# Row groups, PSUM ring and issue orders in the front of a two-layer spectral mixer

## The chip, the cores and the metric

The kernel runs on one core of a Trainium2 chip. The core has TensorE (PE, matrix multiplies), VectorE (DVE), ScalarE (ACT), GpSimd (POOL) and SyncE (SP, which here only issues transfers). The metric is the device time of one execution in microseconds (us), the median of three runs. The profile's span, 346.4 us, runs from the first to the last instruction and is some 2 us shorter than the time of a run.

## The reference

The input x is one sequence of 2048 rows by 512 features in bf16. Two layers follow each other, each of two halves:

```python
x = x + _A_ref(_layernorm(x), A_w_r, A_w_i)      # irfft2(rfft2(x) * W)
x = x + _B_ref(_layernorm(x), B_w1, ..., B_w4)
# _B_ref: h  = gelu(layernorm(x) @ w1)           512 -> 512
#         x1 = x + shifted(h) @ w2               four column groups, shifted by -1, +1, -2, +2 rows
#         y  = x1 + gelu(layernorm(x1) @ w3) @ w4   512 -> 1792 -> 512
```

Both layers use the same weights. The two-dimensional Fourier transforms are done as matrix multiplies with cosine and sine tables.

## The kernel before

**Layout.** A row number of the sequence is written as 16 p + q. The partition is p (128 of them), and q (0 to 15) counts what the code calls a row: a block of 128 x 512. All of x stays on the chip in `x_state`.

**Front.** The first transform needs the normalized x. The mean takes no part in it, except at one frequency, and the scale 1/std of a row is folded into the table: for every row q the engines take statistics (`s`), form mean and variance (`i`), take a square root on ACT for a group of rows (`S`, line 375), invert it on DVE (`J`, line 378), and scale the table T by it (`Q`, line 393 on DVE, line 395 on ACT). PE then multiplies the row with its scaled table (`O`, function `over_p_quarters`, line 424, eight matmuls a row), and a copy takes the result out of PSUM into `V` (`G`, line 157 on DVE, line 159 on ACT). Rows in `ON_ACT` get their statistics from two passes on ACT (lines 363 and 299) and a little arithmetic on GpSimd (`f`, lines 369 to 371); the others from `bn_stats` and `bn_aggr` on DVE (lines 287 and 315). `GROUPS` says which rows share one root. `FIRST` pairs the rows for PE and the copies. Two rows a pair take two PSUM banks; the last two rows go singly, row 15 into two half banks that ACT and DVE empty side by side.

**PSUM.** There are eight banks. In the front `banks` (line 146) hands them out from a ring of six. In the layers every order names its bank after a point (`d0.3` is bank 3), so the ring plays no part there. Zero matmuls (`wake` and `fill`, line 271) in bank 7 keep PE busy before there is data; `WAKE` is how many.

**Layers.** The layers' stages are: second transform step (`d`, line 542 to 548 in layer 1, 553 in layer 2), third step (`q`, 577), the weighting with W on DVE (`p`, 596), the way back (`b` 607, `D` 625, `P` 637), the residual (`a`, 645), layernorm, `w1` (`v`, 677), `w2` (`u`, 693), layernorm, `w3` (`w`, 728), `w4` (`W`, 748), residual (`A`, 754). Before `w1` and `w3` SyncE transposes rows by DMA (`T` and `U`, line 665). Layer 1's last stage already contains the front of layer 2 (`S`, `J`, `Q`, `O`, `G` again).

**Order.** The order is written by hand. `ORDER_0`, `ORDER_A` (layer 1) and `ORDER_B` (layer 2) are lists of such letters with a row, group or pair number and, where there is a choice, V or A for the engine. Each engine takes its own instructions in the order in which the list names them; dependencies between engines become semaphore waits. So moving a letter matters only as against the letters of the same engine, or where it changes who wrote a buffer last.

**Transfers.** SyncE loads x in eight parts and then W; GpSimd loads the tables FL, TL and TR after `f` of group `TABLES` (line 206) and then copies W's rows into the odd partitions, gated by the last scaled table (line 204). Late in the front SyncE queues the MLP weights and layer 2's table FA (line 224), and after layer 1 the table G2 (line 213).

Of the kernel before, what the change touches and what calls it, by code (L numbers as in the profile page):

```python
# [13 lines left out]
BF16 = dt.bfloat16  # L14
# [131 lines left out]
def banks(K, n):  # L146

    k = K.bank
    if k is None:
        k = K.next_bank if K.next_bank + n <= 6 else 0  # L150
        K.next_bank = (k + n) % 6
    return K.ps[:, k:k + n, :]


# [7 lines left out]
def load_all(K, A_x, A_w_r, A_w_i, B_w1, B_w2, B_w3, B_w4):  # L162
    nc = K.nc
    tabs = dft_tables()
    dram = {k: nc.inline_tensor(v, name="tab_" + k).ap() for k, v in tabs.items()}

    def table(k, eng):
        t = K.const.tile(list(tabs[k].shape), BF16, name=k)
        eng.dma_start(t[:], dram[k])
        setattr(K, k, t)  # L170
# [39 lines left out]
        load_TR(1)  # L210

    K.load_tables, K.load_rest = load_tables, load_rest
    K.load_G2 = lambda: nc.sync.dma_start(K.G[:], dram["G2"])

    def load_mlp():
        gate2 = K.const.tile([1, 16], BF16, name="gate2")
        nc.sync.dma_start(gate2[:], K.W[1:2, 1, NH - 1, 1:17])
        for k in ("G", "Tinv"):
            table(k, nc.sync)
        for k, w, n, c in (("w1", B_w1, 4, D), ("w2", B_w2, 4, D), ("w3", B_w3, 4, FH), ("w4", B_w4, 14, D)):  # L220
            t = K.const.tile([P, n, c], BF16, name=k)
            nc.sync.dma_start(t[:], w.rearrange("(t p) n -> p t n", p=P))
            setattr(K, k, t)
        table("FA", nc.sync)

    K.load_mlp = load_mlp
    K.eps = K.const.tile([P, 1], FP32, name="eps")
# [30 lines left out]
def wake(K):  # L258
# [6 lines left out]
    K.zeros = t  # L265
    fill(K, WAKE)


def fill(K, n):
    for i in range(n):  # L270
        K.nc.tensor.matmul(K.ps[:, 7 if K.bank is None else K.bank, 0:256], lhsT=K.zeros[:], rhs=K.zeros[:].unsqueeze(1).to_broadcast([P, 2, P]), start=True, stop=True)
# [126 lines left out]
def over_p(K, qs, split=False):  # L398

    ps = banks(K, 2 if split else len(qs))  # L400
    for i, q in enumerate(qs):
        Tq = K.Tq.pop(q)
        for t in range(2):
            o = ps[:, t, 0:256] if split else ps[:, i, t * 256:(t + 1) * 256]
            a, z = t * P, 256 + t * P
            K.nc.tensor.matmul(o, lhsT=K.x[:, q, a:a + P], rhs=Tq[:, 0:1].to_broadcast([P, 2, P]), start=True,
                               stop=False)
            K.nc.tensor.matmul(o, lhsT=K.x[:, q, z:z + P], rhs=Tq[:], start=False, stop=True)
    return ps
# [53 lines left out]
def first_front(K):  # L463

    new_V(K)
    K.Tq = {}
    at = {q: (g, i) for g, rows in enumerate(GROUPS) for i, q in enumerate(rows)}
    L = [Stats(K, n=len(rows)) for rows in GROUPS]
    for g, rows in enumerate(GROUPS):
        if any(q in ON_ACT for q in rows):  # L470
            L[g].sums()
# [4 lines left out]
    def stats(q):  # L476
        g, i = at[q]
        if q in ON_ACT:
            L[g].mean(i, K.x[:, q, :])
# [22 lines left out]
    def means(g):  # L502
        for i, q in enumerate(GROUPS[g]):
            if q in ON_ACT:
                L[g].from_means(i)
        if g == TABLES:
            K.load_tables()
# [343 lines left out]
PLAIN = 5  # L851
FLEX = "mGnotxY"
ORDER_0 = """
s0 s3 s2 i3 s1 f0 i0 i2 S0 s5 f1 J0 Q0V Q1V Q2A Q3A s4 i4 s6 s7 i6 i7 O0 G0A S1 s10 J1 s12 Q6A s9 Q7V s13 i12 i13 Q4V
s8 S3 O1 G1A Q5V O3 J3 O2 i10 G3A Q12V s11 i8 i11 Q13V O6 f2 S2 J2 G2A Q10V Q11V Q8V O5 G6A Q9A O4 s15 s14 i15 i14 S4
J4 Q14V O7 G5A Q15V G4A O8 G8A G7V G8V
"""
ORDER_A = """
d0.3 t0V d1.6 d2.0 t1A q0.2 x0V p0 t2A q1.4 x1A p1 d4.6 N0 t4A d10.1 t10A q2.4 x2V p2 q4.6 d6.0 x4A t6A d12.3 t12A
d14.5 q10.6 q6.0 d8.2 p4 x10A b4.4 x6V b3.7 d15.6 t8A q8.2 m4A t15A p10 p6 q12.0 b1.4 m3A b0.6 b2.7 x8A x12A b6.2 m2A  # L860
t14V b5.3 m1V p8 q15.0 m0A q14.4 b10.7 x15A b9.6 p12 m6A m10V p15 b8.0 m5A x14A b7.2 m7A b11.3 p14 b12.7 m8V b13.5 m9V
b14.1 m11A m12A b15.2 m13A m14A X4.0 m15A m15V D1.5 Y1A D0.0 Y0A D3.3 Y3A P2.5 a2 s2 P3.6 a3 s3 P0.0 a0 P7.2 P1.7 s0
P6.5 D2.0 a1 s1 a7 s7 r0 a6 s6 Y2V e0 i0 n1V D5.6 Y5A n0V T0 D4.2 Y4A P4.0 a4 P5.4 a5 s4 n3V D7.5 s5 r1 Y7A n2V P11.3
P8.7 c0 a8 a11 e1 i1 n4V n5V T1 P10.4 a10 D6.0 Y6A s8 s10 P15.5 T2 P14.3 n7V n6V s11 P9.2 P12.0 a9 s9 P13.4 c1 v0.1
v1.6 r2 c2 a13 h0 L9 a12 h1 T3 v3.0 a15 n10V s15 v2.5 n11V T5 n8V n9V a14 h3 u0.7 f0 s13 E0 h2 u3.1 T4 s12 f3 E3 u1.6
s14 r3 f1 n15V v5.0 h5 k0 n14A v4.4 h4 n12V n13V T6 u2.7 f2 k2 E2 u4.1 k3 u5.2 f5 c3 u6.0 f6 k1 k6 E1 u7.6 f7 T7 v6.4
f4 h6 R0 o0A o1V U0 o2V v7.3 h7 u13.5 u8.1 u12.6 L12 f8 u10.0 f10 E10 o3A u11.3 U1 f11 E11 E6 u15.7 f12 k7 k12 u9.4
w1.2 E8 f13 g1 L4 k4 E5 f9 E9 w0.0 g0 w5.5 w2.0 g5 w4.5 E13 k5 R1 L13 o5V E4 L10 o6V E7 g2 w3.1 g3 g4 f15 w6.3 g6 k10
W0.2 A0 o7A W3.0 A3 L1 o4A W1.3 A1 U3 U2 w10.1 g10 k8 B1 k9 j1 B3 w7.4 g7 w11.6 W2.0 A2 B2 E15 k11 B0 L3 k13 R2 o10V
o9A o11V w12.2 g12 u14.4 f14 j2 j3 j0 S0 Q0 Q3 g11 w8.0 g8 k14 w9.3 Q1 g9 k15 L8 w13.6 g13 W6.4 A6 U5 W7.2 E12 z0 o8A  # L870
A7 W4.3 U4 w16.4 g16 A4 w15.6 g15 L14 R3 o13V w18.4 g18 w19.0 g19 o12V B4 w14.6 g14 Q2 w20.4 w17.2 W5.6 L6 o15A g20
L11 A5 g17 W9.2 E14 o14V U6 W8.7 O1.3 G1A G1V B5 j5 U7 j4 A8 W10.6 A10 B6 j6 w22.3 g22 B7 W11.0 j7 B8 S1 w24.3 Q5 Q6
A9 B9 g24 j8 L0 L5 O0.1 G0A L2 w23.5 A11 G0V B11 g23 w27.3 j11 B10 g27 w21.6 j10 Q7 g21 j9 w26.3 S2 Q10 g26 w25.1 Q4
Q11 O3.4 g25 Q8 L15 Q9 O2.6 G2A G2V G3A G3V W12.3 A12 B12 j12 S12 W15.6 A15 B15 j15 S15 J15 W13.3 Q15 J12 A13 B13 j13
Q12 W24.4 A24 B24 S13 J13 Q13 W14.5 A14 B14 O4.6 O15.2 G4A j14 S14 G15A G15V O5.4 G5A O6.1 J14 Q14 O14.3 G6A G4V X3.5
G14V X4.0 G14A L7
"""
ORDER_B = """
d15.7 t15V d4.1 t4V d1.3 t1A d8.6 q1.4 x1V t8A p1 q4.2 x4A q15.0 x15V p4 d12.4 t12A d10.6 q8.2 p15 q12.4 t10A x12A
b1.0 d14.1 t14A d2.6 m1A t2A x8V p8 d0.2 p12 b5.5 m5A t0A q10.0 q2.3 x2A x10V p10 d6.5 t6A b9.2 b4.1 b12.0 q14.6 q0.4  # L880
m9A q6.2 m12A p2 m4A b11.0 x0V p0 x6A p6 b2.1 m2A b10.4 x14A b8.2 m8A m10A p14 b3.1 m3A b0.7 m0V b7.5 m11A b13.3 m13A
b14.6 b6.2 m6A m7V m14V b15.4 m15A m15V D3.0 Y3A D2.4 Y2V D1.6 Y1A P6.0 a6 s6 D0.2 Y0A P4.4 a4 s4 P5.5 a5 P7.6 a7 s5
P2.1 P1.4 a2 P0.2 a0 a1 s7 P3.6 a3 r1 D5.0 s2 s0 e1 i1 n5V n4V T2 D7.2 n6V n7V T3 D4.4 Y4V Y5A P11.1 P10.0 a10 s3 s1
r0 Y7A e0 D6.6 i0 P9.5 n2V P8.2 n3V T1 Y6A a11 s10 n0V P14.3 n1A P13.0 P15.7 P12.1 a9 s11 s9 a8 s8 T0 a14 s14 a15 a13
v2.4 r2 v3.2 h3 h2 n9V v1.6 h1 v0.2 u3.5 a12 s12 n8V T4 c0 h0 u1.4 n10V s15 u0.3 c1 n11V f1 f3 T5 s13 f0 E0 k1 k0 r3
n13V u2.6 n15A v5.4 n12V n14V c2 h5 v4.0 f2 E2 E1 u4.5 f4 h4 k4 u7.6 k3 k2 T6 R0 f7 k7 u5.4 f5 u6.7 k5 T7 v6.1 E5 v7.3
h6 h7 o2A o0V E7 o1V c3 u12.2 E3 o3V u8.4 u14.5 f8 u10.1 f14 u15.0 f12 E8 U0 f6 u13.5 f13 k13 U1 w1.3 g1 k8 E6 w5.5 g5
w3.3 E13 k6 f10 g3 w0.1 g0 E14 k10 w6.4 g6 f15 k15 E15 k12 w2.6 g2 k14 w4.4 g4 u11.7 R3 f11 E12 W0.6 o15A o12V o13A
o14V W2.4 U6 u9.1 f9 E9 R1 o5A W3.5 o7V A0 U7 w21.0 w24.6 A3 w27.2 g21 g24 o6A g27 E4 W1.7 A1 w22.2 A2 y2 g22 w26.0
g26 w23.3 g23 z0 w25.6 g25 E10 E11 o4V W12.0 y0 U2 U3 w11.2 g11 w10.6 g10 w13.2 g13 k9 A12 W13.1 k11 R2 o8V o9V o10V  # L890
w7.4 W14.7 A13 w12.2 A14 w9.0 g9 y3 y13 U4 g12 w8.6 g8 W15.1 A15 g7 W4.5 A4 W5.6 A5 y4 y1 W6.3 A6 o11A U5 w14.5 g14 y5
y12 w17.1 g17 y6 w15.4 g15 w18.1 g18 w20.4 g20 w16.0 g16 w19.5 g19 W8.3 A8 y8 W9.2 A9 W7.4 A7 y15 y7 W10.6 A10 y9
W11.5 A11 W20.6 y11 y14 y10 A20 y20
"""


# [28 lines left out]
```

## Time and profile before

Three runs took 348.36, 348.44 and 348.58 us; the median is 348.44 us. The profiled run took 348.18 us.

| engine | busy us | share of the span |
|---|---|---|
| PE | 338.0 | 98% |
| ACT | 198.0 | 57% |
| DVE | 186.0 | 54% |
| POOL | 62.3 | 18% |

A timeline line reads: start, duration, engine, line of the kernel, operation, output tile, input tiles, shapes, how many were merged; in brackets the idle time of the engine before it and what ended that. PE's busy time includes the pipelined ends of matmuls, so successive matmuls overlap in it. A line that merges several instructions gives the time from the first start to the last end. A windows line gives a stretch, its length, then busy us and instruction count of PE, weight loads, DVE, ACT and POOL, the granted share of the PE clock, the busy share of the DMA engines and GB/s.

Where PE stands still: 1.01 us at the start, 1.02 and 0.80 us in the front, 0.21 and 0.16 us as layer 1 begins, some 1.0 us between 180 and 222 us, and from the end of the last matmul, 342.70 us, to the end of the span.

### The profile page before, as it was taken

The page shows a single profiled execution, that of the slowest core. Times are in us where ns is not written, and L with a number is a line of the kernel's source. Part 1 is how long each engine was busy: PE and PEld are TensorE (multiplying, and loading weights), DVE is VectorE, ACT ScalarE, POOL GpSimd, SP SyncE. Part 2 cuts the span into 40 slices and gives each one's busy share as a digit, 9 for nine tenths or more (in the row PEclk, how much of TensorE's full clock was granted, in tenths as well). Part 3 has the DMA queues.
Part 4 walks back from the last instruction along what each step waited for, and adds up shares of the span by engine and source line. Part 5 has one row for each costly group of instructions (what it writes and reads, how often), then busy time and mean ns, then how long its engine had stood idle before and what let it go on. Part 6 is the DMA issues. An engine that isn't in the chain of part 4 may idle for free.

```text
span 346.4 us, 5700 instructions
## 1 busy us (share of the span) xinstructions
PE 338.0 (98%) x2181; PEld 190.4 (55%) x2181; DVE 186.0 (54%) x445; ACT 198.0 (57%) x351; POOL 62.3 (18%) x160
## 2 busy tenths in 40 slices
PE   7999999999999999999999999999999999999995
PEld 5778884444444444444577888444444444444453
DVE  4979597668343451178789969766523110211021
ACT  5989899765616616015537979976581444132500
POOL 2460047520301400010000002653022001000000
PEclk9999999999999999999999999999999999999999
DMA  7987985430030301300000002543003070203002
GB/s 263 285 298 237 383 221 105 78 63 1 3 61 0 62 5 26 62 1 1 2 0 2 2 2 45 101 87 64 10 2 61 0 108 0 45 24 84 0 32 77
DMA packets 45547, 25.12 MB, mean 73 GB/s; under 512 B 34976, under 2 KB 42272, under 8 KB 45520
## 3 DMA queue, kind: packets, MB, share of 16 engines
q1 hardware_dynamic: 44048, 20.27, 24.3%
q0 software_dynamic: 1232, 4.40, 3.7%
q8 instruction: 17, 0.28, 0.3%
q10 hardware_dynamic: 240, 0.10, 0.2%
q14 instruction: 10, 0.08, 0.1%
HBM read 12.13 MB, written 2.10 MB: 41 GB/s over the span
## 4 chain that ended last, share of the span: by engine, by line
PE 80%; DVE 8%; ACT 7%; DMA 2%; issue 2%; DVEq 0%; ACTq 0%
PE ps L748 28%; PE ps L728 28%; PE ps L693 8%; PE ps L677 7%; DVE ln_st L287 2%; PE ps L625 2%; PE ps L607 2%; ACT xn L299 2%; PE ps L637 1%; DVE PB L596 1%; ACT V L159 1%; ACT hT L159 1%; PE ps L577 1%; DVE X L157 1%; ACT X L159 1%
## 5 line engine op out<-in xcount | busy, mean ns | idle before, releaser
L735 ACT ACTIVATE gT<-ps 128x1024 bf16<-128x1024 f32 x56 | 56.7, 1024 | 81.1 <-PE ps L728 80.4
L748 PE MATMUL ps<-w,gT 128*128 128x512 bf16 (+1 forms) x476 | 99.2, 366 | 0.0
L728 PE MATMUL ps<-xT,w 128*128 128x512 bf16 x448 | 99.1, 379 | 0.0
L748 PEld LDWEIGHTS <-gT 128*128 128x128 bf16 x476 | 46.5, 98 | 50.1
L728 PEld LDWEIGHTS <-w 128*128 128x128 bf16 x448 | 43.8, 98 | 52.6
L754 DVE TENSOR_TENSOR x_state<-ps,x_state 128x512 bf16<-128x512 f32 (+1 forms) x34 | 22.2, 657 | 87.0 <-PE ps L748 87.0
L701 DVE SCALAR_TENSOR_TENSOR xn<-xn,ln_c,ps 128x512 bf16<-128x512 bf16 x32 | 23.5, 745 | 27.3 <-PE ps L693 24.1
L693 PE MATMUL ps<-w,hT 128*128 128x512 bf16 x128 | 29.2, 379 | 0.0
L677 PE MATMUL ps<-xT,w 128*128 128x512 bf16 x128 | 28.8, 379 | 0.1
L299 ACT ACTIVATE junk<-xn 128x512 bf16<-128x512 bf16 x32 | 19.9, 622 | 13.3 <-DVE xn L701 13.3
L645 DVE SCALAR_TENSOR_TENSOR x_state<-ps,x_state 128x512 bf16<-128x512 f32 x32 | 20.5, 685 | 4.3 <-PE ps L637 4.1
L287 DVE BATCH_NORM_STATS2 ln_st<-x_state 128x6 f32<-128x512 bf16 (+1 forms) x30 | 19.7, 664 | 3.5 <-DMA x_state<-in_A_x_dram 3.2
L693 PEld LDWEIGHTS <-hT 128*128 128x128 bf16 x128 | 12.4, 98 | 15.3 <-ACT hT L684 0.8
L677 PEld LDWEIGHTS <-w 128*128 128x128 bf16 x128 | 12.4, 98 | 15.3 <-issue 0.7
L305 POOL TENSOR_SCALAR ln_mv<-ln_s 128x4 f32<-128x4 f32 x16 | 5.7, 359 | 82.0 <-DVE x_state L645 68.7
L299 ACT ACTIVATE xn<-x_state 128x512 bf16<-128x512 bf16 x32 | 20.0, 632 | 0.4 <-DVE x_state L645 0.2
L596 DVE TENSOR_TENSOR PB<-X,W 128x2048 bf16<-128x2048 bf16 (+1 forms) x20 | 19.4, 1009 | 0.2
L684 ACT ACTIVATE hT<-ps 128x512 bf16<-128x512 f32 x32 | 17.4, 604 | 2.5 <-PE ps L677 2.4
L307 POOL TENSOR_TENSOR ln_mv<-ln_s,ln_t 128x4 f32<-128x4 f32 x16 | 3.6, 225 | 78.5 <-ACT junk L299 71.4
L607 PE MATMUL ps<-TR,PB 128*128 128x128 bf16 x256 | 16.3, 219 | 0.3 <-DVE X L157 0.3
L159 ACT ACTIVATE TV<-ps 128x1024 bf16<-128x1024 f32 (+1 forms) x16 | 14.2, 913 | 4.0 <-PE ps L553 2.3
L625 PE MATMUL ps<-G,hT 128*128 128x256 bf16 x128 | 15.3, 273 | 0.6 <-ACT hT L159 0.5
(96 smaller groups left out, 389.7 us busy)
## 6 DMA issues: line engine op xcount, KB each, us to landing
w<-in_B_w_dram SPq DMA_DIRECT2D x2, 1792.0 KB, 13.1
W<-W POOLq DMA_DIRECT2D x4, 514.0 KB, 5.5
x_state<-in_A_x_dram SPq DMA_DIRECT2D x8, 256.0 KB, 4.8
out_dram<-x_state SPq DMA_DIRECT2D x15, 128.0 KB, 1.8
w<-in_B_w_dram SPq DMA_DIRECT2D x2, 512.0 KB, 5.4
W<-in_A_w_r_dram SPq DMA_DIRECT2D x7, 128.5 KB, 6.7
W<-in_A_w_i_dram SPq DMA_DIRECT2D x7, 128.5 KB, 6.4
TL<-tab_TL POOLq DMA_DIRECT2D x3, 256.0 KB, 4.8
```

The lines of the kernel that those rows point to most:

```text
L159: K.nc.scalar.activation(dst, src, ACT.Copy, bias=0.0, scale=1.0)
L287: self.K.nc.vector.bn_stats(self.st[i][:, int(k)], src)
L299: K.nc.scalar.activation(out, src, ACT.Square, bias=0.0, scale=D ** -0.5, accum_out=self.s[:, i, 1:2])
L596: nc.vector.tensor_tensor(t, X.pop(u)[:, 0:2 * n].unsqueeze(1).to_broadcast([P, 2, 2 * n, 256]), K.W[:, :, 2 * u:2 * u + 2 * n, 1:257], op ...
L607: nc.tensor.matmul(oh, lhsT=pab[u][:, k, 2 * (b - u) + h, F * P:(F + 1) * P], rhs=K.TR[:, k:k + 2, 2 * b + h], start=(k == 0), stop=(k == 1))
L625: nc.tensor.matmul(o[:, i, e * 256:(e + 1) * 256], lhsT=M[:, F, e, 2 * m + i, :], rhs=K.G[:, F, e, :], start=(F == 0 and e == 0), stop=(F ...
L677: nc.tensor.matmul(o[:, i], lhsT=K.w1[:, t, j * P:(j + 1) * P], rhs=xT[g][:, :, t, :], start=(t == 0), stop=(t == 3))
L693: nc.tensor.matmul(o, lhsT=K.hT[:, j, st:st + P], rhs=K.w2[:, j, :], start=(j == 0), stop=(j == 3))
L701: nc.vector.scalar_tensor_tensor(xn[:, q, :], xn[:, q, :], ln[q // 4].c[:, q % 4:q % 4 + 1], ps.pop(("u", n)), op0=ALU.mult, op1=ALU.add, ...
L728: nc.tensor.matmul(o[:, i], lhsT=K.w3[:, c, t * P:(t + 1) * P], rhs=xT3[g][:, :, c, :], start=(c == 0), stop=(c == 3))
L735: nc.scalar.activation(gT[g][:, 2 * j:2 * j + 2, :], ps.pop(("w", k)), ACT.Gelu_apprx_tanh, bias=0.0, scale=1.0)
L748: nc.tensor.matmul(o, lhsT=gT[g][:, t, i * P:(i + 1) * P], rhs=K.w4[:, t, d], start=(t == 0), stop=(t == 13))
```

## The change

The front gets smaller groups at its start (rows 0 and 1, then 2 and 3), so that a first root does not have to wait for four rows; row 1's statistics go to DVE, so that rows 5 and 9 alone are on ACT. The ring gets all eight banks, so that PE can be one pair further ahead of the copies. Pairs 5 and 6 are copied by DVE and pairs of earlier rows by ACT. Of the zero matmuls three are taken out. The tables FL, TL and TR are loaded after group 2, which now holds rows 4 to 7. FA and G2, layer 2's tables, are each loaded in two halves, one for each of their two index values, so that a reader depends on its half alone. The three orders are written anew; in the two layers' lists most entries keep their places, and the cut diff below shows the moves that touch an engine's own sequence.

```diff
     k = K.bank
     if k is None:
-        k = K.next_bank if K.next_bank + n <= 6 else 0
-        K.next_bank = (k + n) % 6
+        k = K.next_bank if K.next_bank + n <= 8 else 0
+        K.next_bank = (k + n) % 8
...
-    K.load_G2 = lambda: nc.sync.dma_start(K.G[:], dram["G2"])
+
+    def load_G2():
+        for f in range(2):
+            nc.sync.dma_start(K.G[:, f], dram["G2"][:, f])
+
+    K.load_G2 = load_G2
...
-        table("FA", nc.sync)
+        K.FA = K.const.tile(list(tabs["FA"].shape), BF16, name="FA")
+        for t in range(2):
+            nc.sync.dma_start(K.FA[:, t], dram["FA"][:, t])
...
-WAKE = 30
+WAKE = 27
-GROUPS = [[0, 1, 2, 3], [4, 5, 6, 7], [8, 9, 10, 11], [12, 13], [14, 15]]
-ON_ACT = [1, 5, 9]
-TABLES = 1
+GROUPS = [[0, 1], [2, 3], [4, 5, 6, 7], [8, 9, 10, 11], [12, 13], [14, 15]]
+ON_ACT = [5, 9]
+TABLES = 2
...
 ORDER_0 = """
-s0 s3 s2 i3 s1 f0 i0 i2 S0 s5 f1 J0 Q0V Q1V Q2A Q3A s4 i4 s6 s7 i6 i7 O0 G0A S1 s10 J1 s12 Q6A s9 Q7V s13 i12 i13 Q4V
-s8 S3 O1 G1A Q5V O3 J3 O2 i10 G3A Q12V s11 i8 i11 Q13V O6 f2 S2 J2 G2A Q10V Q11V Q8V O5 G6A Q9A O4 s15 s14 i15 i14 S4
-J4 Q14V O7 G5A Q15V G4A O8 G8A G7V G8V
+s0 s1 s3 i1 i0 s2 s4 i3 i2 S0 J0 Q0V s5 i4 S1 J1 Q1A O0 s6 s7 i6 i7 s8 Q2A Q3A O1 f2 S2 J2 i8 Q6V Q7V s9 f3 s10 O3 Q4V
+Q5A s11 O2 G0A i10 i11 s13 S3 G1A J3 Q8V Q10A Q11A Q9V O4 s12 i13 i12 S4 G3A s15 s14 J4 i15 i14 Q12V S5 Q13V G2A G4A
+J5 Q14V O5 Q15V O6 G5V O7 G7A G6V O8 G8A G8V
...
 ORDER_A = """
-... Y7A n2V P11.3 P8.7 c0 ...
+... Y7A n2V P8.7 P11.3 c0 ...
-... u15.7 f12 k7 k12 u9.4 w1.2 ...    W1.3 A1 ...    w7.4 g7 w11.6 W2.0 ...    w21.6 ...
+... u15.7 k7 f12 k12 w1.2 u9.4 ...    W1.4 A1 ...    W2.0 A2 ... w11.6 ...    w21.5 ...
...
 ORDER_B = """
-... D6.6 i0 P9.5 n2V P8.2 ...    u5.4 ...    u12.2 E3 o3V u8.4 u14.5 ...    o15A o12V o13A o14V W2.4 ...
+... D6.6 i0 n2V P8.2 P9.5 ...    u5.3 ...    u14.5 o2A E7 o1V c3 u12.2 ...    o15A o13V o14V W2.4 o12V ...
-... W10.6 A10 y9 W11.5 A11 W20.6 y11 y14 y10 A20 y20
+... W10.6 A10 y10 y9 W11.5 A11 W20.6 y11 y14 A20 y20
```

Besides these, some residual adds (`E`), permutations of W (`L`), norms (`o`) and table scalings (`Q`) change places among DVE's or ACT's instructions of the stages in which PE works through w2, w3 and w4.

## The prediction

> **What bounds the kernel now.** I read the windows by stage first, then the waits of each engine, then the chain of waits inside the stages where TensorE (PE) is not full. The windows view gives start:end, length, and busy us of each engine:
>
> ```profile
> 4.00:20.00 16.00, 13.79 (x148) 11.71 (x147) 13.63 (x45) 13.65 (x29) 7.02 (x17) 1.00 0.99 327
> 20.00:38.00 18.00, 17.96 (x259) 14.95 (x257) 16.80 (x21) 17.17 (x27) 3.87 (x6) 1.00 0.80 272
> 38.00:47.00 9.00, 8.70 (x78) 7.49 (x78) 5.36 (x17) 8.00 (x19) 1.06 (x5) 1.00 1.06 369
> 47.00:180.00 133.00, 133.00 (x688) 65.31 (x687) 78.79 (x206) 67.82 (x120) 26.72 (x63) 1.00 0.19 35
> ```
>
> From 47 to 180 us PE never stops: orders of VectorE (DVE) and ScalarE (ACT) there can save nothing, only create a wait. Where the change can pay is the front, 4 to 20 us, in which PE, DVE and ACT are all at about 85%, none full. DVE's timeline shows its idle times in brackets, with what ended them:
>
> ```profile
> 6.79 0.18 DVE L378 RECIPROCAL ln_r<-ln_r 128x4 f32<-128x4 f32 x1 [0.43 <-ACT ln_r L375]
> 14.53 0.18 DVE L378 RECIPROCAL ln_r<-ln_r 128x4 f32<-128x4 f32 x1 [0.25 <-ACT ln_r L375]
> 17.19 0.17 DVE L378 RECIPROCAL ln_r<-ln_r 128x2 f32<-128x2 f32 x1 [0.36 <-ACT ln_r L375]
> 18.67 1.15 DVE L157 CAST V<-ps 128x512 bf16<-128x512 f32 x2 [0.72 <-PE ps L424]
> ```
>
> PE's timeline of the front:
>
> ```profile
> 7.34 2.80 PE L424 MATMUL ps<-Tq,x_state 128*128 128x256 bf16 x32 [1.02 <-DVE Tq L393]
> 10.94 8.36 PE L424 MATMUL ps<-Tq,x_state 128*128 128x256 bf16 x96 [0.80 <-ACT Tq L395]
> 19.51 0.22 PE L542 MATMUL ps<-xT,V 128*128 128x128 bf16 x1 [0.21 <-ACT V L159]
> 19.88 0.23 PE L544 MATMUL ps<-xT,V 128*128 128x128 bf16 x1 [0.16 <-DVE V L157]
> ```
>
> So from 10.94 PE runs its last 12 rows almost without a gap, 8.1/12 = 0.67 us a row, and DVE waits 0.72 us for it at the end. The layer begins at 19.88, when the last DVE copy out of PSUM is done. The number to forecast is that moment, and what later waits do with it. At the other end stands the store:
>
> ```profile
> 337.45 6.28 SPq L758 DMA_DIRECT2D out_dram<-x_state  x6
> 342.74 0.42 DVE L754 TENSOR_TENSOR x_state<-ps,x_state 128x256 bf16<-128x256 f32 x1 [0.84 <-PE ps L748]
> ```
>
> The last add ends at 343.16; taken one by one, the last three issues before the final one start at 341.93, 342.31 and 342.79 (row 10's first half), and the final store at 343.33.
>
> [...] full clock is recorded from 4.85 us on, through idle times of 1.02 and 0.80 us; no longer idle stands in it. [...] Banks 6 and 7 are not in the front's ring before (bank 7 takes only the zero matmuls), so the longer ring needs nothing else.
>
> **The change part by part.**
>
> *Rows 0 and 1.* Row 1's statistics move from ACT (two passes, 1.23 us of its queue from 4.17) to DVE. DVE start-to-start times, from its timeline: statistics 0.60 (15.33 to 15.94), aggregate 0.10, scaling of T 0.20, reciprocal 0.08, or 0.21 if its scaling follows at once; a 128x1024 copy from PSUM lasts 1.22 us, so 1.14 less the 0.08 overlap of neighbours. These reproduce a stretch without waits: from 7.40 to the last scaling at 14.02 are 8 statistics, 8 aggregates, 2 reciprocals, 4 scalings: 6.56 us against 6.62.
>
> *DVE's new sum.* 14 statistics 8.40, 14 aggregates 1.40, six reciprocals (three of each kind) 0.87, ten scalings 2.00, two whole copies (pairs 5 and 6, before on ACT) 2.28, the half row at the end 0.43: 15.38 us. Before: 13 statistics, 13 aggregates, five reciprocals, twelve scalings, a 512 and a 256 copy: some 13.5 us of work plus 1.76 us of waits and short tails. DVE thus gets 1.9 us more work and must lose its waits. Walking its queue: statistics of 0, 1, 3 from 4.17; of 2 at 6.18; of 4 at 6.78, when its load (landed 6.45) is there; the first reciprocal at 7.58, its ACT root done at 6.64; row 0's scaling 7.79 to 8.07. Reciprocal 1 at 8.1 (ACT root 7.76 to 8.06, behind row 5's two passes). Reciprocal 2 at 10.2, 3 at 12.98, 4 at 15.59: each root is ready before. Reciprocal 5 waits about 0.1 us: row 14's aggregate ends 15.93, root 16.03 to 16.33. Scalings 14 and 15 at 16.6 and 16.8, copies at 17.0 and 18.15, last copy 19.2 to 19.65. Without any wait 4.17 + 15.38 = 19.55.
>
> *PE.* Row 0 starts at about 8.1, not 7.34. At 0.66 us a row: rows 0 to 3 end at 10.7 (row 1 waits for ACT's scaling to 8.5); rows 6, 7 from 10.76; row 4 from 12.07; row 8 from 13.5 (scaled at 13.44); rows 10, 11 to 16.1; rows 12 to 15 from 16.13 to 18.8, against about 19.2 now. The later start is thus regained, since row 6 comes at 10.76 where now the second run starts at 10.94.
>
> *ACT.* Two rows of passes 2.5, six roots 1.2, six scalings at 0.41 2.5, five whole copies at 0.92 4.6, a 512 and a 256 copy about 1.0: 11.8 us against about 13. Walked, it ends near 19.2 (19.38 now). Its copies free the ring in time: bank 2 at 13.7 for a pair ready at 14.8, bank 4 at 15.7 for 16.13, bank 6 at 17.15 for 17.45, bank 0 at 18.06 for 18.1; the last is a tie. With six banks pair 4 would wait for pair 0's copy and so on by one pair earlier; this is what the ring buys, and it is in the walk.
>
> **Front: last copy ends at 19.65 instead of 19.82: -0.2 us**, bounds 19.4 (PE end 18.8 + 0.2 + 0.43) and 19.9 (0.1 us of wait at each of three more roots).
>
> *27 zero matmuls.* At full clock each takes 0.109 us, so they end 0.33 us earlier; PE then idles to 8.1, some 2.0 us. [...] I take 0 and keep 1.5.
>
> *Tables on GpSimd after means 2.* Row 5's second pass ends at 7.9 us in both orders (it is group 1 before and group 2 after), so the loads issue at 8.7 as now. The turn of TL waits for the last scaling, 17.0 instead of 17.95, and lasts 2.6: ready at 19.7, needed at 21.0. Zero.
>
> *20 to 47 us.* I sorted both orders by engine: up to the first back_p the sequences of PE, DVE, ACT and GpSimd are the same; only the interleaving in the text moves. So the stage should shift whole. The doubled W for row pair 0 lands at 21.07 and is used at 22.41; the table work ahead of it issues no later. -0.2 passes through.
>
> *FA in two loads.* SyncE's queue:
>
> ```profile
> 33.38 8.22 SPq L169 DMA_DIRECT2D FA<-tab_FA  x1
> 41.70 1.70 SPq L518 DMA_TRANSPOSE xT<-zeros  x1
> 47.40 12.72 SPq L665 DMA_TRANSPOSE xT<-xn  x6
> ```
>
> The issue of FA blocks for 8.22 us, and behind it stand the dummy transpose and the first transposes of the layer, for which w1(0) at 52.7 waits. A second issue like Tinv's costs 0.47 us and the slack is 47.40 - 43.40 = 4 us: zero. If the second blocked until the weights have landed (48.2), the transposes would slip 2 to 3 us and w1(0), whose second transpose lands at 52.3, by 2 us. G2's second load adds 0.5 us at 145, with the next transpose at 213: zero.
>
> *Orders of the layers.* PE: back_p 8 before 11, w3 swaps, one w2 earlier, two other banks; no operation added. Their producers are done: over 45 to 346 us PE's own waits in the trace sum to 1.0 us, none at these places. In layer 2 norm3 of row 13 goes from ACT (0.80) to DVE (0.41): transpose 6 earlier, but its pair lands at 264.8 and w3(21) starts at 267.0, so hidden. Zero, bounds ±0.3.
>
> *Last stores.* Row 10's half store leaves the place before the final one (issue 0.45). The final store can go when its add is done, 343.16 + 0.04, not at 343.33: -0.13.
>
> **Sum:** 348.44 - 0.2 - 0.13 = 348.1 us.
>
> **The rivals.** (a) *PE sets the front's end and DVE's waits vanish fully*, with better filled ACT queues in 20 to 38 us, where ACT is at 95%: -0.4 there, -0.13 at the tail and another 0.4 from 20 to 47, 347.5. For it: DVE's four waits; against: the later orders are the same by engine. (b) *DVE becomes the bound and loses*: each group of two rows makes its own trip DVE, ACT, DVE of about 0.7 us (6.06 to 7.00); if two of the six are exposed as the three now are, +0.7 - 0.2 - 0.13, and a tie on bank 0 adds 0.2: 349.0. (c) *A stall*: [...] blocked FA, 349.8 to 350.2; against it [...] 4 us of slack.
>
> **How the numbers follow.** The forecast has 0.58, (a) 0.23, (b) 0.12, (c) 0.07. The range 347.4 to 348.9 holds the forecast with its bounds, (a) and the nearer half of (b). Faster by over 0.7 us (0.2%): (a) and a little of the forecast, 0.26; slower by over 0.7: most of (b) and (c), 0.17; the rest, 0.57, is within.
>
> **What would show it.** DVE without brackets from 4.17 to the last copy; PE's first row at 8.1 and last at 18.8; L544 first at about 19.7; 20 to 47 us shifted whole; final store at 343.2 less the shift. Wrong if PE rows of the front take 1.3 us, if a transpose waits behind FA, or if a PE wait appears between 47 and 180 us.

## The result, and the profile after

The change makes the kernel a little faster: 347.34 us (median of 6, 347.02 to 347.96) against 348.51 us for the kernel before beside it (6, 348.17 to 349.55). The ratio is 0.9962, with a 95% interval of 0.9945 to 0.9979, so 1.17 us were gained where 0.34 were forecast. A further series, `after_b`, gives the same size: 0.9961 (0.9949 to 0.9974). In another, `after_again`, 11 executions at the full clock of TensorE have a median of 347.32 us, but 10 had a mean granted clock of 0.993 to 0.995 and took 1.5 us longer; over these 21 the ratio is 0.9981 (0.9969 to 0.9993), so there the change is worth about half as much. (One more execution of that series, at a clock of 0.75, took 443.23 us and is left out.) The lower clock of 0.993 to 0.995 came in 17 of 71 executions with the new front on that chip, in none of 112 with the old front there, and, `after_ring6` apart, in none of 37 with the new front on the three other chips of the experiments.

The windows of the same four stages, in the changed kernel (columns as before):

```profile
4.00:20.00 16.00, 13.76 (x146) 11.75 (x145) 15.06 (x47) 11.81 (x27) 7.29 (x15) 1.00 0.98 324
20.00:38.00 18.00, 17.94 (x258) 14.82 (x255) 16.84 (x21) 17.32 (x27) 2.86 (x5) 1.00 0.90 306
38.00:47.00 9.00, 8.76 (x79) 7.63 (x80) 5.49 (x16) 8.00 (x19) 1.06 (x5) 1.00 0.97 321
47.00:180.00 133.00, 132.58 (x682) 65.39 (x688) 78.91 (x207) 67.69 (x120) 27.87 (x63) 1.00 0.19 34
```

In the first line VectorE (DVE) goes from 13.63 to 15.06 busy us of 16 and ScalarE (ACT) from 13.65 to 11.81: work has moved from ACT to DVE, and DVE is now nearly full. In the other three lines the busy times of VectorE and ScalarE differ by at most 0.15 us and those of PE by at most 0.42 of 133, so whatever came later cannot be seen in busy time. DVE's timeline of the front has one bracket before the last copy of V, the wait for x at its start:

```profile
4.42 1.88 DVE L294 BATCH_NORM_STATS2 ln_st<-x_state 128x6 f32<-128x512 bf16 x3 [3.47 <-DMA x_state<-in_A_x_dram]
...
16.98 2.68 DVE L157 CAST V<-ps 128x1024 bf16<-128x1024 f32 x3
20.21 0.69 DVE L157 CAST TV<-ps 128x512 bf16<-128x512 f32 x1 [0.54 <-PE ps L555]
```

The four waits that stood there before (0.43, 0.25, 0.36, 0.72 us) are gone. TensorE (PE) has one unbroken run of 128 matmuls:

```profile
1.01 5.37 PE L278 MATMUL ps<-zeros 128*128 128x256 bf16 x27 [1.01 <-DVE zeros L269]
8.19 10.95 PE L431 MATMUL ps<-Tq,x_state 128*128 128x256 bf16 x128 [1.80 <-DMA x_state<-in_A_x_dram]
19.48 0.22 PE L549 MATMUL ps<-xT,V 128*128 128x128 bf16 x1 [0.35 <-ACT V L159]
19.72 0.23 PE L551 MATMUL ps<-xT,V 128*128 128x128 bf16 x1
```

SyncE's queue, where FA is now two issues in one line:

```profile
32.46 9.34 SPq L231 DMA_DIRECT2D FA<-tab_FA  x2
41.90 1.20 SPq L525 DMA_TRANSPOSE xT<-zeros  x1
47.25 12.88 SPq L672 DMA_TRANSPOSE xT<-xn  x6
```

**Where the time came from.** When x arrives is not in the kernel's hands: the first statistics start anywhere from 4.08 to 4.50 us over the traces of this study. So stages are compared by their own lengths. Both columns are from traces in which w1's first product does not wait for a transpose: the kernel before, and `after_look2`, the changed kernel in a further execution.

| stretch | before, us | after, us | difference |
|---|---|---|---|
| first statistics to the end of V's last copy | 15.65 | 15.24 | -0.41 |
| from there to the first back_d product | 18.39 | 18.39 | 0.00 |
| first back_d product to w1's first product | 14.52 | 14.40 | -0.12 |
| w1 to the first product with FA | 130.52 | 130.50 | -0.02 |
| FA to layer 2's first back_d product | 20.04 | 19.83 | -0.21 |
| from there to the end of the last add | 139.87 | 139.98 | +0.11 |
| last add to the issue of the final store | 0.17 | 0.03 | -0.14 |
| issue to landing of that store | 1.60 | 1.54 | -0.06 |
| landing to the end of the span | 1.48 | 1.23 | -0.25 |
| sum | 342.24 | 341.14 | -1.10 |

The remaining 0.07 of the measured 1.17 us is less than the scatter of the medians; executions in which w1 has to wait for its transposes, which the next sections show, come on top of the table. The +0.11 was not followed; over the traces of the same two sets of orders that stretch takes 139.80 to 140.07 us. Of the kernels below five are parts of the change, eight alter something in it or in the kernel before, and five are repeats.

### The profile page after: what moved, and what is told of

It is laid out like the page before. It is cut to its first block, busy times and chain, and to the rows that moved or that the text cites. A ratio compares the mean times of both kernels' runs of the same rounds, so it can differ in the third digit from the quotient of the medians.

```text
span 345.6 us, 5672 instructions
## 1 busy us (share of the span) xinstructions
PE 336.6 (97%) x2161; PEld 190.3 (55%) x2178; DVE 187.5 (54%) x448; ACT 195.5 (57%) x348; POOL 62.8 (18%) x157
## 4 chain that ended last, share of the span: by engine, by line
PE 83%; ACT 7%; DVE 5%; DMA 3%; issue 2%; SPq 0%; ACTq 0%; DVEq 0%
PE ps L735 28%; PE ps L755 28%; PE ps L700 8%; PE ps L684 7%; PE ps L431 3%; PE ps L632 2%; PE ps L614 2%; ACT xn L306 2%; PE ps L644 1%; ACT hT L159 1%; DVE PB L603 1%; PE ps L584 1%; ACT X L159 1%; DVE X L157 1%; DVE x_state L652 1%
## 5 line engine op out<-in xcount | busy, mean ns | idle before, releaser
L644 PE MATMUL ps<-Y,Tinv 128*128 128x256 bf16 x128 | 15.4, 272 | 0.5 <-ACT Y L159 0.2
```

## Experiments: the parts of the change

**The kernel before once more** (`same_again`; no edit).

> The kernel before, unchanged. All theories: within 0.1 us of it in the median. How far single runs and the arrival of the first rows of x (4.17 us before, 4.42 us after) scatter says how much of the 1.17 us between the two medians can be chance: if single runs differ by 0.5 us and more, only medians of several runs count.

348.48 us against 348.57, ratio 0.9997 (0.9988 to 1.0006). Its trace holds the surprise of the study. PE's timeline, and SyncE's queue of the same trace:

```profile
50.55 2.47 PE L637 MATMUL ps<-Y,Tinv 128*128 128x256 bf16 x20
53.83 2.53 PE L677 MATMUL ps<-xT,w 128*128 128x512 bf16 x11 [0.81 <-DMA xT<-xn]
```

```profile
34.00 8.03 SPq L169 DMA_DIRECT2D FA<-tab_FA  x1
42.13 1.70 SPq L518 DMA_TRANSPOSE xT<-zeros  x1
47.53 7.00 SPq L665 DMA_TRANSPOSE xT<-xn  x4
```

Here w1's first product waits for its transpose, which in the trace that the prediction read it did not. The same kernel has both. Of 176 executions of the kernel before beside the experiments, 78 took over 348.75 us, up to 350.35, and the rest 348.0 to 348.75.

**The front alone** (`front_only`): groups, ring of eight, `ORDER_0`, `ON_ACT`, `TABLES` and 27 zero matmuls from the change; tables in one load and layers' orders from before.

```diff
-WAKE = 30
-GROUPS = [[0, 1, 2, 3], [4, 5, 6, 7], [8, 9, 10, 11], [12, 13], [14, 15]]
+WAKE = 27
+GROUPS = [[0, 1], [2, 3], [4, 5, 6, 7], [8, 9, 10, 11], [12, 13], [14, 15]]
...  (with the ring of eight and ORDER_0)
```

> The kernel before with the changed front alone: new groups, row 1's statistics on DVE, ring of eight banks, 27 zero matmuls, table loads after group 2, new ORDER_0. Tables in one load, both layers' orders as before. Theory A (the prediction's sum): the last copy of the front 0.2 us earlier for an equal arrival of x, so -0.2 us. Theory B (the front is worth more, because DVE loses all its waits): -0.4 to -0.9 us. Theory C (the layers' orders carry it): 0 to -0.2 us here. In the trace: no idle brackets on DVE from the first statistics to the last copy.

347.88 us, ratio 0.9974 (0.9963 to 0.9984). DVE's and PE's timelines:

```profile
4.08 1.88 DVE L287 BATCH_NORM_STATS2 ln_st<-x_state 128x6 f32<-128x512 bf16 x3 [3.12 <-DMA x_state<-in_A_x_dram]
...
16.64 2.69 DVE L157 CAST V<-ps 128x1024 bf16<-128x1024 f32 x3
```

```profile
7.85 10.95 PE L424 MATMUL ps<-Tq,x_state 128*128 128x256 bf16 x128 [2.30 <-DVE Tq L393]
```

From 4.08 to 19.32 us, the end of the last copy, are again 15.24 us. The front's part is therefore -0.41 us, and it is whole in this kernel. The gain of 0.69 us in the medians is larger than that. Against those executions of the kernel before that took at most 348.75 us it is 0.59; this trace has 0.16 us of it at the other end of the kernel, from the last store's landing to the end (1.32 us instead of 1.48), which nothing in the edit explains. The other 0.10 is the long group: none of these seven executions belongs to it (347.60 to 348.07), beside 16 of 45 of the kernel before.

**The layers' orders alone** (`layers_only`): `ORDER_A` and `ORDER_B` from the change, all else from before.

```diff
-... Y7A n2V P11.3 P8.7 c0 ...      (ORDER_A; with the other moves of both lists)
+... Y7A n2V P8.7 P11.3 c0 ...
```

> The kernel before with the new ORDER_A and ORDER_B alone, the new place of row 10's half store included. Theory A: -0.13 us, all of it at the last store. Theory B: the same. Theory C: -0.4 to -0.7 us, with a part of it between 180 and 222 us, where the trace after is 0.2 us further ahead at 195 us than at 183 us.

347.97 us, ratio 0.9982 (0.9975 to 0.9989), the size that theory C gave, although its trace has a wait of 0.73 us before w1:

```profile
50.47 2.35 PE L637 MATMUL ps<-Y,Tinv 128*128 128x256 bf16 x20
53.54 2.75 PE L677 MATMUL ps<-xT,w 128*128 128x512 bf16 x12 [0.73 <-DMA xT<-xn]
```

Apart from the last store, two stretches are shorter in it: the 20 back_p products before w1 take 2.35 us instead of 2.46, since the old order had one product 0.22 us after its predecessor instead of 0.11 (the trace records no wait there, and why was not tried); and layer 2's third step, which the next kernel singles out.

**The last stores, and one pair of copies** (`tail_and_x10`): two moves in `ORDER_B`.

```diff
-... q10.0 q2.3 x2A x10V p10 ...      A10 y9 W11.5 A11 W20.6 y11 y14 y10 A20 y20
+... q10.0 x10V q2.3 x2A p10 ...      A10 y10 y9 W11.5 A11 W20.6 y11 y14 A20 y20
```

> The kernel before with two small edits of ORDER_B: row 10's half store placed before row 9's store, and x10V named before x2A (two copies on different engines, so no engine's own sequence changes; only which of two rotating buffers each takes, and the waits that follow). Theory A: last store 0.13 us earlier, nothing at 195 us. Theory C: besides, the copy x10V starts 0.2 us earlier after the product before it, without a wait for ACT, and all after it moves by 0.1 to 0.2 us: -0.3 us in all.

348.12 us, ratio 0.9988 (0.9978 to 0.9997). The store now goes 0.03 us after the last add instead of 0.17:

```profile
342.89 0.42 DVE L754 TENSOR_TENSOR x_state<-ps,x_state 128x256 bf16<-128x256 f32 x1 [0.84 <-PE ps L748]
343.34 0.33 SPq L758 DMA_DIRECT2D out_dram<-x_state  x1
```

The copies are the second half. x10V is DVE's, x2A is ACT's, so the swap changes neither engine's own sequence, only which of the two is named first. DVE's timeline of layer 2, before and then with the swap:

```profile
191.72 2.37 DVE L596 TENSOR_TENSOR PB<-X,W 128x2048 bf16<-128x2048 bf16 x2
194.22 1.23 DVE L157 CAST X<-ps 128x1024 bf16<-128x1024 f32 x1
195.48 2.37 DVE L596 TENSOR_TENSOR PB<-X,W 128x2048 bf16<-128x2048 bf16 x2
```

```profile
192.08 2.37 DVE L596 TENSOR_TENSOR PB<-X,W 128x2048 bf16<-128x2048 bf16 x2
194.37 1.22 DVE L157 CAST X<-ps 128x1024 bf16<-128x1024 f32 x1
195.62 2.37 DVE L596 TENSOR_TENSOR PB<-X,W 128x2048 bf16<-128x2048 bf16 x2
```

The second columns are durations of merged instructions; read the starts. Before, the copy begins 2.50 us after the products, 0.13 us past their end; with the swap 2.29 us after, overlapping them. The X buffers rotate and go to the copies in the order in which these are named. Named second, x10V got the buffer that DVE's own product p12 was just reading, and waited for that product to finish (in the trace the semaphore of that product releases it); named first, it gets a buffer free for longer, and ACT's x2A takes the other and waits instead, which ACT can afford. That is 0.21 to 0.23 us, in every kernel that has the swap and in no other.

**The tables' loads alone** (`tables_only`): FA and G2 in two loads each.

```diff
-        table("FA", nc.sync)
+        for t in range(2):
+            nc.sync.dma_start(K.FA[:, t], dram["FA"][:, t])
...  (G2 likewise)
```

> The kernel before with FA and G2 loaded in two halves each, nothing else. If two more issues on SyncE shift the semaphores that its transfers take in turn, so that the last store's comes last in SyncE's closing list (no further waits after it, where the kernel before has two, of 0.06 us each): 0.1 to 0.15 us less than the kernel before, from the store's landing to the end about 1.35 us instead of 1.46 to 1.48. If that list has another cause: the same as before. If the second issue of FA holds the transposes up: 0.3 us or more longer, and a larger share of executions near 349.2 us.

348.35 us against 348.73, ratio 0.9989 (0.9978 to 0.9999). From the last store's landing to the end of the span it takes 1.34 us; in six traces with the loads of before it took 1.46 to 1.48 (1.32 in `front_only`, whose closing barrier is the shortest of all, 0.71 us). SyncE closes with a fixed list of semaphore waits, 0.06 us each. In the kernel before the final store's semaphore is the third from the end of that list, so two waits still follow its landing; with the two more loads that semaphore is the list's last. So the split does save 0.13 us, though by chance and at the other end of the kernel. No transpose was held up: the two issues end at 43.44 us, the first transpose goes at 47.51. The median falls by more than that, 0.38 us, because only 2 of the 13 executions took over 348.75 us, beside 17 of 35 of the kernel before: whether the split itself makes the long executions rarer was not tried further. The remaining 0.12 us of the 0.25 in the table lie in the closing barrier (0.86 us before, 0.74 after, but 0.87 in `after_row1_act`, which has the change's tail), and stay unexplained.

**The ring alone** (`before_ring8`): the kernel before with eight banks.

```diff
-        k = K.next_bank if K.next_bank + n <= 6 else 0
-        K.next_bank = (k + n) % 6
+        k = K.next_bank if K.next_bank + n <= 8 else 0
+        K.next_bank = (k + n) % 8
```

> The kernel before with eight PSUM banks in the front's ring instead of six, its groups and orders as they are. The changed kernel with six banks took 4 us longer because a product waited 2.2 us for a copy that stood behind other work on ScalarE. If the eight banks are only what the new row order needs, and not a gain of their own: within 0.2 us of the kernel before, with the last copy 15.6 us after the first statistics as in it. If the old order also waited for banks: 0.3 us less or more, and a front of 15.3 us or less.

348.63 us, ratio 1.0002 (0.9990 to 1.0014), the front 15.56 us. In the old order the ring brings nothing.

## Experiments: what the change leans on

**Six banks in the changed kernel** (`after_ring6`): the same edit backwards.

> The changed kernel with the ring of six banks again. Both theories: pair 5 waits for the copy of pair 3 and pair 6 for that of pair 2, so the last copy of the front ends 0.4 to 1.0 us later after the arrival of x (15.6 to 16.2 us instead of 15.24), and the time rises by as much, to 347.8 to 348.4 us; if the ring were worth nothing, 347.4.

351.98 us, ratio 1.0088 (1.0062 to 1.0114), far more than expected. PE's timeline:

```profile
7.91 5.44 PE L431 MATMUL ps<-Tq,x_state 128*128 128x256 bf16 x64 [1.04 <-DMA x_state<-in_A_x_dram]
15.55 1.50 PE L431 MATMUL ps<-Tq,x_state 128*128 128x256 bf16 x16 [2.21 <-ACT V L159]
17.44 5.49 PE L431 MATMUL ps<-Tq,x_state 128*128 128x256 bf16 x48 [0.38 <-ACT V L159]
```

The ninth row waits 2.21 us for a bank that an ACT copy has to empty. Then the rows themselves slow down: 16 matmuls took 1.36 us before the wait (5.44 / 4), and the last 48 take 5.49 where 4.1 would do. The windows of the same trace show why, in the third column from the right, the granted clock:

```profile
14.00:16.00 2.00, 0.45 (x6) 0.50 (x7) 1.34 (x6) 2.00 (x5) 0.00 (x0) 1.00 0.94 302
16.00:18.00 2.00, 1.62 (x17) 1.28 (x15) 2.00 (x9) 1.83 (x5) 0.00 (x0) 0.72 1.04 394
18.00:20.00 2.00, 2.00 (x15) 1.56 (x13) 0.53 (x3) 1.68 (x2) 1.21 (x2) 0.50 1.07 361
```

The missing bank thus cost twice, by the wait of 2.21 us and by the granted clock of 0.50 that followed it (all four executions have a mean clock of 0.989 to 0.995), and the front takes 19.25 us instead of 15.24. The ring is no gain by itself, but the new row order can't do without it.

**Eight zero matmuls in the changed kernel** (`after_wake8`), **and 36** (`after_wake36`).

```diff
-WAKE = 27
+WAKE = 8        (after_wake36: 36)
```

> The changed kernel with 8 zero matmuls instead of 27: they end at about 2.8 us, so PE idles for over 5 us before the first row. If the clock falls or never rises in between, rows of the front take 1.3 us instead of 0.66 [...]; if idling is harmless, no change. It says what the zero matmuls buy and whether three fewer could have mattered.

> The changed kernel with 36 zero matmuls instead of 27, which end at about 8.2 us (27 took 5.37 us, 0.199 us each), just as the first product becomes ready. If the gap of 1.80 us is what brings the lower clock: all executions near 347.3 us with a clock of 0.999 or more. If not: the same two groups as the changed kernel. If nine more push the first product back: 0.1 to 0.2 us more in all of them.

With eight: 350.39 us, ratio 1.0045 (1.0030 to 1.0060). PE's timeline:

```profile
1.01 1.89 PE L278 MATMUL ps<-zeros 128*128 128x256 bf16 x8 [1.01 <-DVE zeros L269]
7.96 12.03 PE L431 MATMUL ps<-Tq,x_state 128*128 128x256 bf16 x128 [5.06 <-DVE Tq L400]
```

The 128 matmuls take 12.03 us instead of 10.95, and the front 16.32 instead of 15.24: +1.08. Another 1.44 us are a wait of PE at 70.9 us for a transpose that took 4.85 us to land instead of about 3.2; why it did is not known. With 36 zero matmuls the gap before the first product is 0.29 us, the 128 take 10.94 us, and the time is 347.29 us, ratio 0.9965 (0.9952 to 0.9977), the changed kernel's. So a gap of 1.80 us cost nothing in these executions. They ran on a chip on which the changed kernel showed no lower clock either, so they don't tell whether the gap brings it where it appears.

**The changed kernel four more times** (`after_again`, `after_b`, `after_look1`, `after_look2`; no edit).

> The changed kernel once more, as the measure for the three beside it. If the four terms that the traces show (front 0.4 us, the buffers of layer 2's x10V and x2A 0.22 us, the last store 0.14 us, and the transposes that no longer wait behind the weights, 0 to 1.1 us from run to run) are the whole of it, 347.3 to 347.7 us, all of its runs within 1 us of each other, where the kernel before spreads over 348.2 to 349.4 us. A rival in which the front alone carries the change: 347.9 to 348.2 us.

> The changed kernel once more. If the two groups belong to it: executions near 347.3 us at a mean clock of 1.000 and others near 348.8 us at 0.994, about half of each, none between. In a trace of the second group the granted clock is at half speed for 4 us or so somewhere (0.006 of 346 us is 2 us lost). If the gap of 1.8 us before the first product is the cause, that place is 8 to 20 us; if it lies in the layers, it is elsewhere. If the earlier second group was the chip's alone: all near 347.3 us.

> The changed kernel, one look: 347.3 us at a clock of 1.000, or 348.8 us at 0.994; in the second case the trace shows where the clock is low.

> The changed kernel, one look: 347.3 us at a clock of 1.000, or 348.8 us at 0.994; in the second case the trace shows where the clock is low.

347.28 us (`after_b`, 347.07 to 347.95), 347.77 and 347.19. None had the lower clock, so where in the program it sits is open. The loss of 1.5 us would fit one stretch of half clock of the kind seen in `after_ring6`; that is an estimate from that trace (3.41 us at a clock of 0.50 do the work of 1.7 us), not shown by one of these executions.

**Row 1's statistics back on ACT** (`after_row1_act`), **and the tables moved behind row 9's variance as well** (`after_row1_tab3`).

```diff
-ON_ACT = [5, 9]
+ON_ACT = [1, 5, 9]
-s0 s1 s3 i1 i0 s2 s4 i3 i2 S0 J0 Q0V s5 i4 S1 J1 Q1A O0 s6 ...
+s0 s3 s1 f0 i0 s2 i3 i2 S0 J0 Q0V S1 J1 Q1A s5 s4 i4 O0 s6 ...
-TABLES = 2      (after_row1_tab3 only)
+TABLES = 3
```

> The changed kernel with row 1's statistics on ACT again (where the trace after shows ACT idle until 6.48 us), its group of two kept, the root of rows 2 and 3 ahead of row 5's passes. DVE loses 0.7 us of work. Walked: the first row on PE at about 7.1, DVE 0.4 us ahead from row 6 on, the last copy 14.8 us after the arrival of x instead of 15.24: -0.4 us against the changed kernel, 346.9 us. If DVE no longer bounds the front, PE does, and less than 0.2 us comes.

> Row 1's statistics back on ScalarE and rows 0 to 3 first, as in the earlier run of that, and GpSimd's four table loads moved behind row 9's mean and variance. In the earlier run the first row's product started 0.87 us sooner (7.13 against 8.19 us, with x 0.18 us sooner), and all of that was gone at 12.7 us, where ScalarE's square root for rows 8 to 11 waited 0.45 us; GpSimd's three small instructions for row 9 stood behind the table loads until 12.68 us. If that queue is what gave the gain back: the square root at about 12.25 us, the last copy 14.8 to 15.1 us after the first statistics instead of 15.24 to 15.42 us, and 0.3 to 0.4 us less than the changed kernel. If VectorE's own sum of work sets the front's end, whichever rows it takes: less than 0.15 us. If the tables now come late for the turn and for TR (first products with TL at 21.1 us): slower.

The first: 347.64 us, ratio 0.9968 (0.9957 to 0.9978); no gain over the changed kernel can be told, and the front is 15.42 us. PE's first product came 2.89 us after the first statistics instead of 3.77, but the root for rows 8 to 11 came 8.48 us after them instead of 8.24. ACT's timeline and GpSimd's:

```profile
12.72 0.30 ACT L382 ACTIVATE ln_r<-ln_mv,eps 128x4 f32<-128x4 f32 x1 [0.45 <-DVE ln_st L294]
```

```profile
11.15 0.74 POOL L189 DMA_DIRECT2D TR<-tab_TR  x1
11.90 0.21 POOL L376 TENSOR_TENSOR ln_mv<-ln_s 128x1 f32<-128x1 f32 x1
12.19 0.19 POOL L377 TENSOR_TENSOR ln_mv<-ln_s,ln_mv 128x1 f32<-128x1 f32 x1
12.47 0.21 POOL L378 TENSOR_SCALAR ln_mv<-ln_mv 128x1 f32<-128x1 f32 x1
```

The profile puts ACT's wait down to DVE's statistics. GpSimd's last instruction for row 9 ends at 12.68 us, just before the root, and stands behind four table loads; ACT's passes for row 9 were done by 11.0. The second kernel shows that it was GpSimd: with the loads behind it the root starts at 12.20 us without a wait, and the front takes 14.98 us, 0.27 less than the changed kernel. But the loads now come late:

```profile
21.64 0.50 PE L584 MATMUL ps<-TV,TL 64*128 64x256 bf16 x6 [0.72 <-POOL TL L255]
...
26.31 0.22 PE L549 MATMUL ps<-xT,V 128*128 128x128 bf16 x1 [0.49 <-DVE X L157]
```

and at the first product of the next step (28.71 us), counted from the first statistics, it is 1.2 us behind the changed kernel: 348.27 us, ratio 0.9990 (0.9974 to 1.0006).

## Experiments: the transposes behind the weights

**w4 and FA after layer 1's transposes for w1 and w2**, in the kernel before (`w4_late`) and in the changed one (`after_w4_late`); **FA alone after layer 1's last transpose** in the changed one (`after_FA_late`).

```diff
-        for k, w, n, c in (("w1", B_w1, 4, D), ("w2", B_w2, 4, D), ("w3", B_w3, 4, FH), ("w4", B_w4, 14, D)):
+        for k, w, n, c in (("w1", B_w1, 4, D), ("w2", B_w2, 4, D), ("w3", B_w3, 4, FH)):
...
+        if op == "T7" and not last:
+            K.load_late()      # w4, FA;  after_FA_late: FA alone, at U7
```

> The kernel before, with the loads of w4 and FA (2.0 MB) issued after layer 1's last transpose for w1 instead of ahead of its first one. In the traces so far the first product of w1 starts 0.1 us after the product before it, or up to 1.1 us later, and then the first transposes landed late, behind these loads. Theory T (the front pays a second time, because it moves these loads ahead of the transposes): the wait before w1 is at most 0.15 us here, single runs no longer reach 349 us, the median falls by 0.2 to 0.4 us. Theory F (only the front's own 0.4 us counts, the wait before w1 is something else): no change.

> The changed kernel with the loads of w4 and FA issued after the last of layer 1's transposes before w1 and w2, instead of before the first of them. If the change has gained by getting the first transposes clear of those loads, nothing is left to gain here: within 0.25 us of the changed kernel, and no wait before w1's first product. If the transposes still wait for the weights in some runs of the changed kernel: 0.3 to 0.6 us less than it, and a smaller spread. If w4 or FA now come late for their own readers (first product with w4 at 81 us, with FA at 183 us): slower by more than 0.5 us.

> The changed kernel with FA's two loads issued after layer 1's last transpose (143.7 us) instead of ahead of its first; FA is read at 183 us. In the changed kernel FA lands last of what stands ahead of the first transpose, 1.1 to 3 us after w4 counted over the two halves. If the transposes wait for the whole of the transfers ahead: no wait before w1's first product, all executions between 346.9 and 347.4 us, a median 0.1 to 0.2 us under the changed kernel's 347.3. If w4 alone is enough to hold them: as the changed kernel, with some executions near 347.9. If FA now comes late or its loads disturb G2's: 0.5 us or more longer, with a wait at 183 us.

In the kernel before, 348.06 us, ratio 0.9974 (0.9968 to 0.9980), and all 21 executions within 347.80 to 348.45: the long group is gone (beside it 24 of 34 of the kernel before took over 348.75 us), and the median falls by 0.89 us where theory T gave 0.2 to 0.4. SyncE's queue shows the dummy transpose issued early, at 33.43 us (it landed at 43.20, instead of 49.98), and the late loads at 68 us:

```profile
33.43 1.21 SPq L522 DMA_TRANSPOSE xT<-zeros  x1
47.72 12.73 SPq L669 DMA_TRANSPOSE xT<-xn  x6
...
68.32 0.58 SPq L227 DMA_DIRECT2D w<-in_B_w_dram  x1
68.95 0.93 SPq L169 DMA_DIRECT2D FA<-tab_FA  x1
```

In the changed kernel the same move is a loss: 348.51 us, ratio 0.9998 (0.9985 to 1.0012), 1.2 us over the changed kernel. There is no wait before w1, but PE's timeline has a new one:

```profile
79.76 1.90 PE L739 MATMUL ps<-xT,w 128*128 128x512 bf16 x8 [1.12 <-DMA xT<-xn]
```

Its `ORDER_A` has w3 start before the last four w2 products, so its transposes are needed earlier, and they stand behind the loads issued at 68 us. Moving FA alone to where nothing is due avoids that: 347.25 us, ratio 0.9963 (0.9953 to 0.9973), with 18 executions at 347.0 to 347.66 and four at the lower clock. No wait before w1; the median of those 18 is 347.2, about 0.1 under the changed kernel, too little to tell apart.

How the traces of these kernels divide (the one at a clock of 0.75 left out): the transfer just ahead of the first transpose is the dummy one, which stands behind w4 and FA where these are not moved. In the six traces in which it landed after 50.3 us (`same_again`, `layers_only`, `before_ring8`, `after_b`, `after_look1`, `after_row1_tab3`), the first transpose's issue took 2.48 to 2.88 us, and w1's first product came 0.68 to 0.97 us late (the brackets alone show 0.52 to 0.81). In the thirteen in which it landed by 50.0 us that issue took 1.26 to 2.24 us, and w1 was late once, by 0.21 us. In `same_again` the three landed in the order of their issue: w4 at 48.62 us, FA at 50.79, the dummy at 51.04. No run here shows what makes the dummy land late: with FA landed by 49.01 us it came at 50.64, with FA at 49.76 it came at 49.98. No run moves the dummy transpose alone, so how much of the wait is its own is open.

## Why the prediction fell short

The direction was right, and the mechanism of the front; of the gain of 1.17 us, 0.34 were forecast. Of the 1.10 us in the table the front has 0.41 where 0.2 was forecast, the layers' orders 0.24 where zero was taken (0.12 + 0.02 + 0.21 - 0.11), the last store 0.20 where 0.13 was forecast, and the closing of the kernel 0.25, which no step looked at. So the step that failed is the zero for the layers' orders, taken from PE's waits alone; the front was mis-sized by 0.2, and the close was missing from the sum. Term by term:

- **The front, -0.2: right in kind, half the size.** Counted from the first statistics, the prediction put the last copy at 15.48 us (19.65 - 4.17), against 15.65 before; it came at 15.24. Its sum of DVE's work, 15.38 us, was 0.14 too large, and the other 0.10 are waits that it added and that did not come. That the last copy ended at 19.66 us on the clock, where 19.65 was forecast, is luck: in that trace x arrived 0.25 us later than before.
- **PE's rows:** the first came 3.77 us after the first statistics, where 3.9 was forecast, and the last product ended 14.71 us after them, where 14.6 was. **What the ring buys:** right in kind, but "one pair earlier" understates it, 4.0 us in the front of `after_ring6`. **Tables on GpSimd, 0:** right for this order; `after_row1_act` shows how close GpSimd's queue is.
- **Zero matmuls, 0:** right for the executions at full clock. They did not end 0.33 us earlier but 0.06 later (6.38 us instead of 6.32), since full clock is recorded from 5.66 us in that trace and from 4.85 us before; so PE idled 1.80 us. Whether this gap brings the lower clock of some executions is open.
- **"So the stage should shift whole."** From V's last copy to the first back_d product it did: 18.39 us in both.
- **"FA in two loads ... the slack is 4 us: zero."** The split does no harm, as said. But the slack was read from one trace in which nothing waited. The same queue, unchanged, makes w1 0.7 to 1.0 us late in other executions of either kernel, and `w4_late`, which takes w4 and FA (and with them the late dummy transpose) out of the way, ends that. This wait was missing from the sum, though not from what would have shown the prediction wrong. What the change does to it is less sure. Counted from the first statistics, the weights' loads go out some 1.4 us earlier with the new front (at 25.4 to 26.6 us instead of 27.0 to 27.6, over the traces with either front as it stands), because GpSimd's work that they wait for starts at the last scaled table, and that comes 1.1 us earlier. Long executions are rarer with it, but not clearly: over 348.75 us are 23 of 68 of the kernel before in the series beside the changed kernel's, and over 347.65 us, 1.10 lower, 4 of 25 of the changed kernel at full clock.
- **"the sequences of PE, DVE, ACT and GpSimd are the same; only the interleaving in the text moves."** This step was used for layer 1, and layer 2's moves were then all costed at zero by PE's waits. It fails for buffers that rotate: the name order decides who gets which. 0.21 us, `tail_and_x10`. The 0.12 us of the back_p order lay within the bound of 0.3, but its value taken was zero: a product that follows 0.22 us after its predecessor shows as no wait in the timeline, so from 47 to 180 us PE seemed never to stop.
- **Last stores, -0.13:** -0.14 for the issue, as said. A further 0.06 is the final store's own issue (0.33 us instead of 0.40, with none just ahead of it), and 0.13 the closing list.
- **The rivals.** (a) had nearly the right time, 347.5, in part by luck: its -0.4 for a front in which DVE waits nowhere is right, but it has nothing of layer 2 and the closing, and its -0.4 from 20 to 47 us did not come. (b) was right that DVE becomes the bound of the front, which has no idle time left (15.06 busy us of 16); it was wrong that the trips to the roots would be exposed. (c), a stall, did appear as a lower mean clock, 0.993 to 0.995 in executions of one chip and 1.5 us longer, but not as the rule; the 1.5 us that the prediction kept beside its 0 for the zero matmuls was its author's estimate, and no trace of that time showed such a loss.

## What to carry to other kernels

Measure a stage as a length from its own first event, and before calling a queue's slack safe look at more than one execution: the spread of the times, 348.0 to 350.35 us for the kernel before, was the sign that a wait came and went. When an order written by hand is compared by engine, compare also the order in which rotating buffers are asked for (0.21 us in `tail_and_x10`). And an early bulk load is not free because its data are needed late: ask what is queued behind it on the same issuing engine, also at the place to which one moves it (the same move of w4 and FA gained 0.89 us in the median of `w4_late` and brought a wait of 1.12 us in `after_w4_late`).

## What was unexpected of the hardware

TensorE's clock does not follow from the length of one idle gap. Gaps of 1.80 us (the changed kernel) and 2.30 us (`front_only`) before the first product left the 128 matmuls at 10.95 us, while one of 2.21 us in the middle of `after_ring6` was followed by half clock. The traces record when the clock changes: in `after_ring6` full clock begins at 6.64 us, half clock at 16.88 and full clock again at 20.30, so after 10.24 and 3.41 us. In the 3.41 us before the fall PE was busy for 1.32 us. In the changed kernel, where the clock did not fall, the 3.41 us from its rise at 5.66 us hold the gap and 1.60 us of work:

```profile
13.47:16.88 3.41, 1.32 (x16) 1.32 (x17) 2.22 (x8) 3.41 (x7) 0.00 (x0) 1.00 0.98 322
16.88:20.29 3.41, 3.03 (x21) 2.25 (x19) 1.75 (x10) 2.63 (x4) 1.50 (x2) 0.50 1.05 370
```

```profile
5.66:9.07 3.41, 1.60 (x19) 1.31 (x17) 3.38 (x14) 2.59 (x9) 0.97 (x4) 1.00 1.01 380
```

In `front_only` full clock begins at 3.95 us, and the 3.41 us from there, too, have 1.60 us of work. But there the 3.41 us up to the first product hold the whole gap of 2.30 us, so 1.11 us of work at most, less than before the fall in `after_ring6`, and the clock did not fall. What decides when it falls is not shown.

When full clock begins differs from execution to execution: at 3.68 to 6.94 us in the traces with 27 or more zero matmuls. No trace was taken of an execution of the changed kernel at the mean clock of 0.993 to 0.995, so neither the place nor the cause of the lower clock is shown, nor why one chip alone has such executions.

In `after_wake8` the first full clock on record begins at 10.69 us, and the eight zero matmuls started 0.21 us apart, against 0.11 at full clock: PE ran at the slower pace before its idle time of 5.06 us as well. The windows view counts the time ahead of the first record as 1.00, so there it is the pace of the matmuls that tells the clock.
